# Query projections of two batches as three float32r products, with a transfer plan at another rate and a new order list

## The chip, the core and the metric

The kernel runs on one NeuronCore of a Trainium2 chip, as one program with one launch. Five engines work side by side: TensorE (PE in the profile, with its weight loads shown apart as PEld), VectorE (DVE), ScalarE (ACT), GpSimd (POOL) and SyncE (SP), which here only issues transfers. The metric is the device time of one execution in microseconds (us). Three runs of the kernel before gave a median of 582.48 us (582.31 to 582.5); the execution that was profiled took 582.31 us.

## The reference

Three layers follow each other. All inputs and outputs are float32.

```python
# 1. attention with random features: 4 batches, 8 heads, 576 positions, head size 64, 128 features
def phi(x):                                   # x = q or k, scaled by 64 ** -0.25
    h = x @ omega.T - (x * x).sum(-1, keepdims=True) / 2
    return np.exp(h - h.max(-1, keepdims=True)) / np.sqrt(128)
kv, z = phi(k).T @ v, phi(k).sum(0)           # for each batch and head
x = (phi(q) @ kv) / (phi(q) @ z + 1e-6)       # heads side by side: 2304 tokens x 512
# 2. dense layer, 512 -> 2048 -> 512
h = x @ w_in
x = (h * np.clip(h + 3, 0, 6) / 6) @ w_out
# 3. eight experts, 512 -> 1024 -> 512: each token with x @ w_skip > 0 goes to its best one
out[t] = x[t] + gate[t] * (np.maximum(x[t] @ w1[e], 0) @ w2[e])
```

The change touches the product of q with omega inside phi(q).

## The kernel before

**Attention.** Heads are taken in pairs: a pair (b, p) is batch b and two heads, one in partitions 0 to 63 and one in 64 to 127, so there are four pairs in a batch. For each pair the keys are projected in blocks of 128 positions (`nat`, L448), reduced to their maximum on DVE (L454), passed through the exponential on ACT (L469) and multiplied with v (`k_kv`, L485). The queries are projected with the features in the partitions (`q_proj`, L515): two halves of 288 columns each, and in each half two float32 matmuls, one for each head, of which one uses the array's upper 64 rows and the other its lower 64. One float32 matmul of the program stands as two MATMUL records in the trace. ACT copies the result to SBUF (L543), POOL takes the maximum over partitions (L551), DVE subtracts it (L556), ACT takes the exponential (L560), and TensorE multiplies with kv (`x_num`, L570). DVE divides (L581 to L583), TensorE transposes (L592), ACT and DVE split the result into a high and a low float32r part, `xh` (L607) and `xl` (L612).

**Dense layer.** Tokens go in five chunks of 512, 512, 256, 512 and 512. For each chunk and each of 16 slices of the hidden layer `mm1` (L712) makes three products of high and low parts, twelve float32r matmuls, and `mm2` (L743) three more for each 128 tokens. Batch 0 must be through before the first `mm1`; batches 1, 2 and 3 are worked in between the matmuls of chunks 0 to 2. In the same time ACT and DVE turn the 64-bit words in which the weights arrive into float32 and split them (L643 to L690).

**Experts.** A large block for one expert (L990 to L1072), a small one (L1157 to L1192) and a loop for what is left, which runs zero times on these inputs.

**Array modes.** TensorE runs in three ways here: over the whole array (`mm1`, `mm2`, transposes, and the fill matmuls on `idle`, L299), in two halves of 64 rows (L448, L515), and in parts of its columns (L485, L570, L1169, L1192). A change between these is called a mode change below.

**What sets the order.** All work is registered as some 2,000 numbered operations, each with an engine, a cost, a due time, what it reads and writes, and the tiles it takes from small pools. The stored list ORDER says in which order they are written into the engines' queues, and each engine works its queue in that order. `Schedule.gaps` walks the list with the planned costs; in the kernel itself its result only decides how many fill matmuls are put into the planned idle time of TensorE before projections of batch 0. The constants DMA and RATE are its latency in us and its bytes per us for transfers. The tile pool "raw" has three buffers of 576 columns, which hold k and q of the pair in work and what is loaded ahead. SP works its queue in order, so that a load which waits for a buffer holds up those behind it.

Of the kernel before, what the change touches and what calls it, by code (L numbers as in the profile page):

```python
# [51 lines left out]
MERGE = 2  # L52
VX = 2
# [200 lines left out]
def performer_moe_kernel(  # L254
# [1026 lines left out]
    def act(n):  # L1281
        return 0.09 + n * 0.84e-3
# [16 lines left out]
    def attention(b, start, period):  # L1299
        for p in range(4):  # L1300
# [12 lines left out]
            def kind(tag):  # L1313
                return "ps"
# [335 lines left out]
```

## Time and profile before

| what | value |
|---|---|
| median of 3 runs | 582.48 us |
| profiled execution, its own time | 582.31 us |
| its span, first to last instruction | 580.5 us |
| TensorE matmul busy | 565.8 us, 97% |
| VectorE busy | 423.6 us, 73% |
| ScalarE busy | 293.4 us, 51% |
| GpSimd busy | 109.4 us, 19% |
| mean granted TensorE clock | 0.993 of full speed |
| instructions in the span | 11189 |

The span is 1.8 us shorter than the execution's own time, since that includes what lies around the first and the last instruction. Matmul busy time is modelled up to the end of each matmul's pipeline, so a record of 0.39 us may follow the one before it by 0.23 us; what a matmul costs is read from the distance between starts.

### The profile page before, as it was taken

The page shows a single profiled execution, that of the slowest core. Times are in us where ns is not written, and L with a number is a line of the kernel's source. Part 1 is how long each engine was busy: PE and PEld are TensorE (multiplying, and loading weights), DVE is VectorE, ACT ScalarE, POOL GpSimd, SP SyncE. Part 2 cuts the span into 40 slices and gives each one's busy share as a digit, 9 for nine tenths or more (in the row PEclk, how much of TensorE's full clock was granted, in tenths as well). Part 3 has the DMA queues.
Part 4 walks back from the last instruction along what each step waited for, and adds up shares of the span by engine and source line. Part 5 has one row for each costly group of instructions (what it writes and reads, how often), then busy time and mean ns, then how long its engine had stood idle before and what let it go on. Part 6 is the DMA issues. An engine that isn't in the chain of part 4 may idle for free. (4 is left out here: it accounts for less than half of the span.)

```text
span 580.5 us, 11189 instructions
## 1 busy us (share of the span) xinstructions
PE 565.8 (97%) x4117; PEld 469.5 (81%) x4117; DVE 423.6 (73%) x1116; ACT 293.4 (51%) x665; POOL 109.4 (19%) x83
## 2 busy tenths in 40 slices
PE   9899999999999999999999999999999999999993
PEld 7778788888888787878988888888888888898872
DVE  5999999988752442356678886798898974599961
ACT  5999999896563533357743431321432224553310
POOL 4543023000020202023222000020020133200363
PEclk9999999999999999999999999999999999999997
DMA  8635665666565143214644243121123535274721
GB/s 318 223 106 165 204 218 180 209 194 222 159 238 153 37 137 119 60 48 129 180 144 146 74 124 101 48 92 56 35 32 112 148 92 164 84 235 126 237 65 66
DMA packets 37256, 79.52 MB, mean 137 GB/s; under 512 B 5612, under 2 KB 6252, under 8 KB 37200
## 3 DMA queue, kind: packets, MB, share of 16 engines
q1 hardware_dynamic: 35024, 74.80, 41.1%
q0 software_dynamic: 1744, 3.56, 2.1%
q8 instruction: 33, 0.54, 0.4%
q10 hardware_dynamic: 432, 0.43, 0.3%
q14 instruction: 23, 0.19, 0.1%
HBM read 63.71 MB, written 15.18 MB: 136 GB/s over the span
## 5 line engine op out<-in xcount | busy, mean ns | idle before, releaser
L743 PE MATMUL acc<-wo,gh 128*128 128x512 f32 x576 | 180.9, 395 | 0.0
L743 PEld LDWEIGHTS acc<-wo,gh 128*128 128x128 f32 x576 | 105.4, 188 | 22.3 <-issue 1.2
L763 DVE CUSTOM_DVE_ANT_0 idle<-x,wg 128x512 uint8<-128x512 f32 x162 | 112.6, 695 | 5.3 <-ACT x L749 1.5
L743 PE MATMUL acc<-wo,gl 128*128 128x512 f32 x288 | 112.3, 390 | 0.0
L551 POOL PARTITION_ALL_REDUCE mx<-pr x26 | 52.9, 2074 | 237.6 <-ACT pr L543 237.6
L727 ACT CAST gh<-g 128x512 fp32r<-128x512 f32 (+1 forms) x80 | 46.6, 584 | 97.7 <-PE acc L743 84.2
L733 DVE TENSOR_TENSOR gl<-g,gh 128x512 fp32r<-128x512 f32 (+1 forms) x80 | 51.2, 640 | 58.0 <-ACT gh L727 22.0
L718 ACT ACTIVATE g<-mm,half_t 128x512 f32<-128x512 f32 (+1 forms) x80 | 52.0, 650 | 67.5 <-DVE gl L733 36.1
L712 PE MATMUL mm<-xh,wih 128*128 128x512 f32 (+1 forms) x320 | 80.8, 374 | 0.5 <-DVE xn L583 0.5
L712 PE MATMUL mm<-xl,wih 128*128 128x512 f32 (+1 forms) x320 | 78.8, 368 | 0.0
L723 DVE SCALAR_TENSOR_TENSOR g<-g,mm 128x512 f32<-128x512 f32 (+1 forms) x80 | 49.7, 630 | 26.1 <-ACT g L718 25.8
L712 PEld LDWEIGHTS mm<-xh,wih 128*128 128x128 f32 x320 | 56.0, 188 | 12.1 <-DVE xn L583 0.7
L712 PEld LDWEIGHTS mm<-xl,wih 128*128 128x128 f32 x320 | 56.8, 188 | 10.2
L743 PEld LDWEIGHTS acc<-wo,gl 128*128 128x128 f32 x288 | 54.0, 188 | 11.6
L712 PE MATMUL mm<-xh,wil 128*128 128x512 f32 (+1 forms) x256 | 61.7, 363 | 0.0
L712 PEld LDWEIGHTS mm<-xh,wil 128*128 128x128 f32 x256 | 44.8, 189 | 7.9 <-DMA wil<-wils 0.4
L841 POOL DMA_INDIRECT tab<-rec,r_sloti x18 | 19.5, 1086 | 154.9 <-DVE rec L837 151.0
L469 ACT ACTIVATE kp<-att,kmx 128x128 f32<-128x128 f32 x130 | 38.4, 395 | 7.8 <-DVE kmx L454 6.7
L454 DVE TENSOR_REDUCE kmx<-att 128x3 f32<-128x384 f32 (+1 forms) x64 | 28.9, 484 | 12.8 <-PE att L448 12.6
L556 DVE TENSOR_TENSOR pr<-pr,mx 128x576 f32<-128x576 f32 x26 | 26.1, 1005 | 1.4 <-POOL mx L551 1.3
L668 DVE CUSTOM_DVE_ANT_0 ca<-w,ca 128x1024 uint16<-128x1024 uint16 x32 | 23.6, 741 | 3.0 <-ACT w L654 2.1
L448 PEld LDWEIGHTS att<-wb,raw 64*128 64x128 f32 x260 | 20.3, 195 | 5.6 <-ACT pr L543 1.5
(222 smaller groups left out, 777.3 us busy)
## 6 DMA issues: line engine op xcount, KB each, us to landing
wil<-wils SPq DMA_DIRECT2D x64, 256.0 KB, 2.7
w<-w_in SPq DMA_DIRECT2D x16, 512.0 KB, 4.0
w<-w_out SPq DMA_DIRECT2D x16, 512.0 KB, 3.8
out<-x SPq DMA_DIRECT2D x18, 256.0 KB, 3.6
x1d<-x SPq DMA_DIRECT2D x18, 256.0 KB, 3.8
vx<-vn SPq DMA_DIRECT2D x13, 322.5 KB, 4.5
wils<-cl SPq DMA_DIRECT2D x16, 256.0 KB, 4.2
wraw<-w SPq DMA_DIRECT2D x16, 256.0 KB, 2.9
```

The lines of the kernel that those rows point to most:

```text
L454: V.reduce_max(out=mx[:, 0:n], in_=st[key, b, p, g, h][:, 0:n * M].rearrange("p (g m) -> p g m", m=M), axis=AX.X, negate=True)
L469: A.activation(kp[:, i], ps[:, i * M:(i + 1) * M], AF.Exp, bias=mx[:, i:i + 1], scale=1.0)
L551: G.partition_all_reduce(mx, st["e", b, p, r], channels=128, reduce_op=bass_isa.ReduceOp.max)
L556: V.tensor_sub(pr, pr, st.pop(("qm", b, p, r)))
L668: V.tensor_tensor(c, c, lo, op=ALU.add)
L712: T.matmul(po, w[:, k, :], moving(x, k, c), start=(n == 0), stop=(n == 3 * KC - 1))
L718: A.activation(t, mmp[c, f][:, 0:CHS[c]], AF.Relu, bias=half_t, scale=2.0 ** -UP / 6.0)
L723: V.scalar_tensor_tensor(out=t, in0=t, scalar=1.0, in1=mmp.pop((c, f))[:, 0:CHS[c]], op0=ALU.min, op1=ALU.mult)
L727: A.copy(gh, gt[c, f])
L733: V.tensor_sub(gl, t, gh.bitcast(F32))
L743: T.matmul(accs[c, t], g[:, ts], w[:, r, f % 2, :], start=(f == 0 and j == 0), stop=(f == FT - 1 and j == 2))
L763: V.tensor_tensor_reduce(out=idle.bitcast(mybir.dt.uint8), in0=x1[i], in1=wg[:, e, :], scale=1.0, scalar=0.0, op0=ALU.mult, op1=ALU.add, a ...
```

## The change

Queries of batches 2 and 3 (`SPLIT = 2`) are projected in another form. ACT rounds omega (`wbh`) and q (`qh`) to float32r, DVE takes the rests (`wbl`, `ql`), and each half projection becomes three float32r products, wbh·qh + wbl·qh + wbh·ql, over 320 and 256 columns instead of 288 and 288. `qh` and `ql` take buffers of the pool "raw", and the load of the next pair's keys is placed behind the making of `ql`. Two constants of the plan change, some small tiles share their memory, and ORDER is another list, with new numbers because there are 18 more operations.

```diff
+SPLIT = 2
 ORDER = """
-256 257 294 295 16 1 332 333 370 258 260 296 259 31 266 268 272 263 273 261 279 274 297 280 262 281 301 298 275 264
...
+256 257 409 294 295 332 333 16 370 258 260 31 296 259 268 1 266 272 269 334 261 273 267 263 262 310 279 311 317 274
...
-    DMA, RATE, TURN, STEP, HOLD = 2.0, 0.2e6, 0.2, 0.03, 0.6
+    DMA, RATE, TURN, STEP, HOLD = 2.4, 0.4e6, 0.2, 0.03, 0.6
...
+    wbh = sm.tile([128, M], F32R, tag="wbh", name="wbh")
+    wbl = od.tile([128, M], F32R, tag="wbl", name="wbl")
...
     def q_cols(b, p, i):
+        if b >= SPLIT:
+            return (slice(0, 320), slice(320, S))[i]
         return slice(i * 384, 384 + i * 192) if (b, p) in QPE else slice(i * HS, (i + 1) * HS)
+
+    def wb_hi():
+        A.copy(wbh, wb)
+
+    def wb_lo():
+        V.tensor_sub(wbl, wb, wbh.bitcast(F32))
+
+    def q_hi(b, p):
+        st["qh", b, p] = at.tile([128, S], F32R, tag="raw", bufs=RAW, name="qh")
+        A.copy(st["qh", b, p], st["qr", b, p])
+
+    def q_lo(b, p):
+        st["ql", b, p] = at.tile([128, S], F32R, tag="raw", bufs=RAW, name="ql")
+        V.tensor_sub(st["ql", b, p], st["qr", b, p], st["qh", b, p].bitcast(F32))
...
-        if (b, p) not in QPE:
+        if b >= SPLIT:
+            qh, ql = st["qh", b, p], st["ql", b, p]
+            for j, (w, x) in enumerate(((wbh, qh), (wbl, qh), (wbh, ql))):
+                for r in range(2):
+                    T.matmul(ps[r][:, 0:n], w[half(r), :], x[half(r), c], start=(j == 0), stop=(j == 2))
+        elif (b, p) not in QPE:
             for r in range(2):
                 T.matmul(ps[r][:, 0:n], wb[half(r), :], qr[half(r), c], start=True, stop=True)
...
-            add("ACT" if b + p == 0 else "SP", SPC, -9, load_k, (), seq="sraw", w=["kr"], tl=[("raw", "k")], nbytes=S * 512)
+            add("ACT" if b + p == 0 else "SP", SPC, -9, load_k, (), seq="sraw", w=["kr"], tl=[("raw", "k")], nbytes=S * 512,
+                aft=[("ql", (b * 4 + p - 1) // 4, (p - 1) % 4)] if b * 4 + p > 4 * SPLIT else [])
...
+            fine = b >= SPLIT
+            if fine:
+                add("ACT", act(S), u, q_hi, (), r=["qr"], w=["qh"], tl=[("raw", 0), ("raw", "h")])
+                add("DVE", dve(S), u, q_lo, (), mode="x", r=["qh", "wbl"], w=["ql"], tl=[("raw", 0), ("raw", "h"), ("raw", "l")])
...
-                add("PE", 0.62, u + i, q_proj, (i,), mode="r", r=["wb", "qr"] + ["qm", "shapes"] * mine, w=[("qps", i)],
+                add("PE", 3 * (n + 32) / 2400 + 0.03 if fine else 0.62, u + i, q_proj, (i,), mode="r", r=["wb", "ql" if fine else "qr"] + ["qm", "shapes"] * mine, w=[("qps", i)],
...
+    sc.add("ACT", 0.22, 90.0, lambda: wb_hi(), r=["wb"], w=["wbh"])
+    sc.add("DVE", 0.2, 90.0, lambda: wb_lo(), mode="x", r=["wbh"], w=["wbl"])
```

Three places show how the order moves. In the changed kernel the same code stands some 3 to 33 lines further down: L472 is the old L469, L488 the old L485, L539 the old L515, L567 the old L543, L594 the old L570, L616 the old L592, L736 the old L712, L767 the old L743, and L536 is the new product.

The first is the start of ACT's queue: `pr` and `lent_h` hold projected queries, `kp` and `lent_r` exponentials of keys, `w` and `ca` weights being turned. Before:

```order
L543 ACT_TABLE_LOAD
L543 COPY pr<-mm 128x288 x3
L469 ACTIVATE kp<-att,kmx 128x128 x3
L543 COPY pr<-mm 128x288
L469 ACTIVATE kp<-att,kmx 128x128 x5
L469 ACTIVATE lent_r<-att,kmx 128x128 x3
L543 COPY lent_h<-mm 128x288
```

And in the changed kernel:

```order
L513 ACT_TABLE_LOAD
L513 CAST wbh<-wb 128x128
L472 ACTIVATE kp<-att,kmx 128x128 x7
L567 COPY pr<-mm 128x288
L567 COPY lent_h<-mm 128x288
L567 COPY pr<-mm 128x288
L567 COPY lent_h<-mm 128x288
L567 COPY pr<-mm 128x288
L567 COPY lent_h<-mm 128x288
L567 COPY pr<-mm 128x288
```

ACT begins with the rounding of omega and seven exponentials of the first pair's keys, where it began with three copies of projected queries; the copies of the first two pairs now alternate.

The second is TensorE's queue just ahead of the first `mm1`, the last products of batch 0 and the first of batch 1. Before:

```order
L570 MATMUL att<-lent_h 64x65 x20
L570 MATMUL att<-kv,pr 64x65 x20
L592 MATMUL mm<-ident,xn 128x128 x5
L515 MATMUL att<-raw,wb 128x288 x2
L448 MATMUL att<-wb,raw 128x128 x6
L515 MATMUL att<-raw,wb 128x288 x2
L448 MATMUL att<-wb,raw 128x128 x6
L712 MATMUL mm<-xh,wih 128x512 x4
```

And in the changed kernel:

```order
L616 MATMUL mm<-ident,xn 128x128 x8
L488 MATMUL att<-vx,kp 64x65 x12
L594 MATMUL att<-kv,pr 64x65 x20
L488 MATMUL att<-vx,kp 64x65 x8
L616 MATMUL mm<-ident,xn 128x128 x4
L539 MATMUL att<-raw,wb 128x288 x2
L451 MATMUL att<-wb,raw 128x128 x6
L539 MATMUL att<-raw,wb 128x288 x2
L736 MATMUL mm<-xh,wih 128x512 x4
```

Twenty more of the narrow products with v (`att<-vx,kp`) now stand ahead of the first `mm1`: 220 narrow products in all against 200, with the same 90 products of L448 and L515 on either side.

The third is TensorE's queue around one pair of batch 2 or 3; `raw`, `qh` and `ql` are queries, `wb`, `wbh` and `wbl` omega. Before:

```order
L570 MATMUL att<-kv,pr 64x65 x20
L743 MATMUL acc<-wo,gh 128x512 x2
L743 MATMUL acc<-wo,gl 128x512
L743 MATMUL acc<-wo,gh 128x512 x2
L743 MATMUL acc<-wo,gl 128x512
L592 MATMUL att<-ident,xn 128x128 x3
L515 MATMUL att<-raw,wb 128x288 x4
L448 MATMUL att<-wb,raw 128x128 x10
L485 MATMUL att<-vx,kp 64x65 x20
L712 MATMUL mm<-xh,wih 128x256 x4
```

And in the changed kernel:

```order
L594 MATMUL att<-kv,pr 64x65 x20
L536 MATMUL att<-qh,wbh 128x320 x2
L536 MATMUL att<-qh,wbl 128x320 x2
L536 MATMUL att<-ql,wbh 128x320 x2
L767 MATMUL acc<-wo,gh 128x512 x2
L767 MATMUL acc<-wo,gl 128x512
L536 MATMUL att<-qh,wbh 128x256 x2
L536 MATMUL att<-qh,wbl 128x256 x2
L536 MATMUL att<-ql,wbh 128x256 x2
L767 MATMUL acc<-wo,gh 128x512 x2
L767 MATMUL acc<-wo,gl 128x512
L616 MATMUL att<-ident,xn 128x128 x3
```

Four matmuls of 288 columns become twelve of 320 or 256, and here the two halves no longer stand together: three wide matmuls of `mm2` lie between them.

Over the whole queue of TensorE there are 83 mode changes before and 94 after; ahead of the first `mm1` there are 21 and 25. The numbers of wide, narrow, transposing and key-projecting matmuls are the same in both kernels, and fill matmuls go from 21 to 16.

## Rows read from the trace of the kernel before

**Rows 1.** The page, busy time of the engines: us, share of the span, instructions.

```profile
PE 565.8 (97%) x4117; PEld 469.5 (81%) x4117; DVE 423.6 (73%) x1116; ACT 293.4 (51%) x665; POOL 109.4 (19%) x83
```

**Rows 2.** Busy time by stage, with granted TensorE clock (1.00 is 2.4 GHz) and transfers.

```profile
core 0: us, PE busy (x) PEld busy (x) DVE busy (x) ACT busy (x) POOL busy (x), PEclk, DMA share, GB/s
0.00:48.00 48.00, 43.59 (x643) 36.40 (x644) 40.01 (x94) 40.99 (x117) 20.57 (x15) 1.00 0.63 217
48.00:130.00 82.00, 81.98 (x591) 66.47 (x592) 75.16 (x152) 77.90 (x156) 13.08 (x6) 1.00 0.61 193
210.00:330.00 120.00, 119.55 (x1129) 101.58 (x1125) 70.36 (x171) 56.77 (x154) 24.14 (x12) 1.00 0.36 108
571.00:580.50 9.50, 0.00 (x0) 0.00 (x0) 0.51 (x1) 0.00 (x0) 1.37 (x2) 0.59 0.15 59
```

**Rows 3.** Waits of TensorE, the up-projection's: us in total, times, longest.

```profile
PE mm L712 <- DVE xn L583: 0.5, 1, 0.5
```

**Rows 4.** TensorE from 222 us: start, us to modelled end, instructions.

```profile
223.40 1.08 PE L712 MATMUL mm<-xh,wil 128*128 128x512 f32 x4
224.41 0.76 PE L515 MATMUL att<-raw,wb 64*128 64x288 f32 x4
225.09 1.39 PE L485 MATMUL att<-vx,kp 128*64 128x65 f32 x40
226.41 1.20 PE L712 MATMUL mm<-xh,wih 128*128 128x512 f32 x4
```

**Rows 5.** TensorE from 289 us.

```profile
291.41 1.24 PE L515 MATMUL att<-raw,wb 64*128 64x288 f32 x8
292.58 0.73 PE L743 MATMUL acc<-wo,gh 128*128 128x512 f32 x2
...
295.25 0.64 PE L712 MATMUL mm<-xh,wil 128*128 128x256 f32 x4
295.73 0.64 PE L712 MATMUL mm<-xh,wih 128*128 128x256 f32 x4
```

**Rows 6.** TensorE from 512 us.

```profile
512.17 0.75 PE L1034 MATMUL mm<-xl,gw 128*128 128x320 f32 x4
512.75 0.75 PE L1034 MATMUL mm<-xh,gw 128*128 128x320 f32 x4
```

**Rows 7.** TensorE from 568 us.

```profile
568.51 0.62 PE L1066 MATMUL acc<-gw,xh 128*128 128x512 f32 x2
568.97 0.39 PE L1066 MATMUL acc<-gw,xl 128*128 128x512 f32 x1
```

**Rows 8.** Weight loads of the up-projection from the page, with the mean ns of one.

```profile
L712 PEld LDWEIGHTS mm<-xh,wih 128*128 128x128 f32 x320 | 56.0, 188 | 12.1 <-DVE xn L583 0.7
```

**Rows 9.** ACT in the first 50 us; idle time before, with its releaser, in brackets.

```profile
7.20 1.00 ACT L543 COPY pr<-mm 128x288 f32<-128x288 f32 x3 [3.58 <-PE mm L515]
...
9.12 1.46 ACT L469 ACTIVATE kp<-att,kmx 128x128 f32<-128x128 f32 x5
10.37 0.97 ACT L469 ACTIVATE lent_r<-att,kmx 128x128 f32<-128x128 f32 x3
...
11.40 0.81 ACT L643 ACTIVATE ca<-w 128x512 f32<-128x512 f32 x1
11.98 0.82 ACT L543 COPY lent_h<-mm 128x288 f32<-128x288 f32 x2
...
38.19 0.62 ACT L469 ACTIVATE lent_r<-att,kmx 128x128 f32<-128x128 f32 x2 [0.89 <-DVE kmx L454]
...
45.15 0.77 ACT L607 CAST xh<-mm 128x384 fp32r<-128x384 f32 x2
```

**Rows 10.** DVE's first maximum of keys.

```profile
5.74 0.76 DVE L454 TENSOR_REDUCE kmx<-att 128x2 f32<-128x256 f32 x2 [1.31 <-PE att L448]
```

**Rows 11.** TensorE at the first up-projection.

```profile
47.88 1.19 PE L712 MATMUL mm<-xh,wih 128*128 128x512 f32 x4
```

**Rows 12.** Loads of keys from the page: KB each, median us from issue to landing.

```profile
raw<-kt SPq DMA_DIRECT2D x12, 288.0 KB, 4.4
```

More of the change, by code (lines that the diff above doesn't have):

```diff
@@ L315, in performer_moe_kernel @@
     V.memset(ones, 1.0)
-    first = const.tile([128, 1], F32, name="first")
-    G.partition_all_reduce(first, idle[:, 0:1], channels=128, reduce_op=bass_isa.ReduceOp.max)
+    upper = const.tile([128, 1], F32, name="upper")
+    G.partition_all_reduce(upper, idle[:, 0:1], channels=128, reduce_op=bass_isa.ReduceOp.max)
     half_t = const.tile([128, 1], F32, name="half_t")
@@ L328, in performer_moe_kernel @@
     pidx = const.tile([128, 1], F32, name="pidx")
-    upper = const.tile([128, 1], F32, name="upper")
     thr = const.tile([128, NT // 128], F32, name="thr")
@@ L361, in performer_moe_kernel @@
     od = ctx.enter_context(tc.tile_pool(name="od", bufs=1))
-    od.tile([128, 56], F32, tag="pad", name="pad")
+    wbh = sm.tile([128, M], F32R, tag="wbh", name="wbh")
+    wbl = od.tile([128, M], F32R, tag="wbl", name="wbl")
+    od.tile([128, 16], F32, tag="pad", name="pad")
     at = ctx.enter_context(tc.tile_pool(name="at", bufs=1))
@@ L811, in route_copy @@
         V.tensor_copy(tot, ps[:, 64:64 + TPC[c] * NE].rearrange("p (n e) -> p n e", e=NE))
-        pos = sm.tile([128, TPC[c], NE], F32, tag="r_pos", name="r_pos")
+        pos = sm.tile([128, TPC[c], NE], F32, tag="r_d", name="r_pos")
         V.tensor_copy(pos, ps[:, 0:TPC[c] * NE].rearrange("p (n e) -> p n e", e=NE))
@@ L818, in route_slot @@
         tot, pos, oh, act = rt["tot"], rt["pos"], rt["oh"], rt["act"]
-        sm_ = sm.tile([128, TPC[c]], F32, tag="r_sm", name="r_sm")
+        sm_ = sm.tile([128, TPC[c]], F32, tag="r_mx", name="r_sm")
         V.reduce_sum(out=sm_, in_=rt["ex"], axis=AX.X)
@@ L868, in list_in @@
         j3 = bc(jdx.unsqueeze(2), LS)
-        exc = sm.tile([128, NE], F32, tag="l_exc", name="l_exc")
+        lw = lb["w"] = sm.tile([128, M], F32, tag="wbh", name="lw")
+        exc = lw[:, 3 * NL:3 * NL + NE]
         V.tensor_sub(exc, inc, nb)
@@ L879, in list_e @@
         ge, lt = lb["ge"], lb["lt"]
-        hit = sm.tile([128, NL], F32, tag="l_hit", name="l_hit")
+        lw = lb["w"]
+        hit = lw[:, 0:NL]
         V.reduce_sum(out=hit, in_=ge, axis=AX.X)
         V.tensor_mul(lt, ge, bc(eidx.unsqueeze(1), LS))
-        ei = sm.tile([128, NL], I32, tag="lb_e", name="lb_e")
-        eb = sm.tile([128, NL], F32, tag="l_eb", name="l_eb")
+        ei = lw[:, NL:2 * NL].bitcast(I32)
+        eb = lw[:, 2 * NL:3 * NL]
         V.reduce_sum(out=eb, in_=lt, axis=AX.X)
@@ L898, in list_r @@
         V.tensor_scalar(hit, hit, -float(TABN), float(TABN), op0=ALU.mult, op1=ALU.add)
-        ri = sm.tile([128, NL], I32, tag="lb_r", name="lb_r")
+        ri = lb["w"][:, 3 * NL + NE:4 * NL + NE].bitcast(I32)
         V.tensor_add(ri, eb, hit)
@@ L1203, in performer_moe_kernel @@
     ntot = sm.tile([128, 1], I32, tag="ntot", name="ntot")
-    ea = sm.tile([128, 1], I32, tag="ea", name="ea")
-    ra = sm.tile([128, 1], I32, tag="ra", name="ra")
-    es = sm.tile([128, 1], I32, tag="es", name="es")
-    rs = sm.tile([128, 1], I32, tag="rs", name="rs")
+    ear = sm.tile([128, 2], I32, tag="ea", name="ear")
+    ea, ra = ear[:, 0:1], ear[:, 1:2]
+    esr = sm.tile([128, 2], I32, tag="es", name="esr")
+    es, rs = esr[:, 0:1], esr[:, 1:2]
     lb = {}
@@ L1253, in list_b @@
         V.tensor_sub(rest, cnt, used)
-        nb = begun(rest, "b_nb")
-        lb["nb"], lb["inc"] = nb, prefix(nb, "b_inc")
+        nb = begun(rest, "a_oh")
+        lb["nb"], lb["inc"] = nb, prefix(nb, "a_t8")
     def expert_of(t):
@@ L1301, in attention, with add @@
             t = start + p * period + AT[f"o{b}{p}"]
-            def add(eng, cost, dt, f, a, r=(), w=(), tl=(), nbytes=0, seq=None, mode="f", over=()):
+            def add(eng, cost, dt, f, a, r=(), w=(), tl=(), nbytes=0, seq=None, mode="f", over=(), aft=()):
                 last = chain.get(seq)
@@ L1308, in add @@
                     chain[seq] = (seq, b, p)
-                sc.add(eng, cost, t + dt, lambda p=p: f(b, p, *a), mode=mode, o=[last] if last else [], r=[k if k in ("wb", "shapes") else (k, b, p) if isinstance(k, str) else (*k, b, p) for k in r],
+                sc.add(eng, cost, t + dt, lambda p=p: f(b, p, *a), mode=mode, o=[*([last] if last else []), *aft], r=[k if k in ("wb", "wbl", "shapes") else (k, b, p) if isinstance(k, str) else (*k, b, p) for k in r],
                        w=[(k, b, p) if isinstance(k, str) else (*k, b, p) for k in w] + list(over),
@@ L1352, in attention @@
                 n = c.stop - c.start
-                add("PE", 0.62, u + i, q_proj, (i,), mode="r", r=["wb", "qr"] + ["qm", "shapes"] * mine, w=[("qps", i)],
-                    tl=[("raw", 0)] + [(kind("x"), "q", r, i) for r in range(2)] + [("pr", r) for r in range(2)] +
+                add("PE", 3 * (n + 32) / 2400 + 0.03 if fine else 0.62, u + i, q_proj, (i,), mode="r", r=["wb", "ql" if fine else "qr"] + ["qm", "shapes"] * mine, w=[("qps", i)],
+                    tl=([("raw", "h"), ("raw", "l")] if fine else [("raw", 0)]) + [(kind("x"), "q", r, i) for r in range(2)] + [("pr", r) for r in range(2)] +
                     ([("qmx", g, h) for g, h in parts] if mine else []))
```

161 rows, old and new, of the table ORDER are left out of this document.

## The prediction

> **What bounds the kernel now.** I read the busy shares first. TensorE is busy for 97% of the span, ScalarE for 51% and VectorE for 73% [rows 1], so the question is where the missing 3% lie, and whether TensorE's time is work or waiting. The chain that ended last is of no help, since it holds only the last two instructions. The table by stage does [rows 2]. The reader is to see that all of TensorE's missing time lies at the two ends: 43.59 of the first 48 us are busy, 81.98 of the next 82, and then nothing is missing but 0.45 us between 210 and 330. After 571 us TensorE has no instruction, and 9.5 us of scatter and closing follow. The granted clock stands at 1.00, the 2.4 GHz level, in every stretch with matmuls. In the first stage ScalarE is busy 40.99 us of 48 and works without a break of more than 0.9 us from 7.20 us on [rows 2, 9]; there TensorE is fed by ScalarE and VectorE. From the first up-projection at 47.88 us [rows 11] on, TensorE is the bound, and its list of waits has only one entry for the up-projections, 0.5 us [rows 3].
>
> So the time is: start of the first up-projection, plus all of TensorE's work that stands behind it, plus waits, plus the tail. A change helps if it makes that work less, moves some of it ahead of 47.88 us, or lets the first up-projection start sooner. Work on other engines is hidden unless it makes TensorE wait.
>
> **The change part by part.**
>
> *The products themselves.* A pair's projection before is eight records in two halves of the array. From their start to the next group lie 291.41 to 292.58, 1.17 us [rows 5]; for four records it is 224.41 to 225.09, 0.68 us [rows 4]. The difference, 0.49 us, is two steps of two records side by side, 0.245 us each, and 0.68 - 0.49 = 0.19 us is what a visit costs beyond its work. A pair thus costs 4 x 0.245 = 0.98 us. The new product has no row. Its columns run in float32r; wide float32r matmuls start 0.145 us apart at 320 columns (512.17 to 512.75, four of them, rows 6) [rows 6] and 0.12 us apart at 256 (295.25 to 295.73, four) [rows 5]. If two heads still run side by side, a pair costs 3 x (0.145 + 0.12) = 0.795 us. Gain 0.185 us for a pair, 8 pairs: **-1.5 us**. Bounds: the fastest float32r row is 0.23 us for 512 columns (568.51 to 568.97, two) [rows 7], 0.45 ns a column, hence 0.776 us for the pair's 3 x 576 columns and -1.6 us. The other end is that the two heads take turns: 1.59 us a pair, +4.9 us. I take -1.5 because the float32 records of the same two halves do run side by side: one after the other, eight of them at 0.245 us would take 1.96 us, not 1.17.
>
> A weight load has a mean of 188 ns [rows 8]. For each head and half projection there are now three, where there were two, one for each record. Wide matmuls with a load each still start 0.12 us apart at 256 columns [rows 5], so loads of 188 ns lie beside the matmul ahead of them. The page "TensorE: Matmul & The Clock Gate" of the Trainium skill, in its Part 3 on packing small matmuls, says that a weight load overlaps with a matmul in flight only when it goes to other rows of the array. In this kernel's wide stream each load goes to the same rows, and it hides almost wholly, so the trace does not bear the rule out for float32r; the case in which it holds is priced among the rivals from the 188 ns.
>
> *Mode changes.* A visit in another mode costs 0.19 us beyond its work (above); the part at the way in shows as well where four wide matmuls after a visit take longer than 4 x 0.23. I counted 83 mode changes before and 94 after, 21 and 25 of them ahead of the first up-projection. Behind it there are 62 and 69, seven more, where the halves of a projection no longer stand together: 7 x 0.19 = **+1.3 us**. Those four ahead of it lie in time that is waited away anyway, if the start is set by ScalarE.
>
> *Work moved across the first up-projection.* Twenty narrow products now stand ahead of it. As 40 records they took 225.09 to 226.41, 1.32 us [rows 4], less 0.19 for the visit: 1.1 us that TensorE no longer does later, **-1.1 us**, if the up-projection doesn't start later for it.
>
> *The start.* ScalarE's last cast of batch 0 that the first up-projection needs begins at 45.15 and ends at 45.92 us [rows 9]. In the new order ScalarE has more ahead of that cast: six exponentials of keys of batch 1 at 0.25 us (five in 9.12 to 10.37) [rows 9], one scaling of weights at 0.58 (11.40 to 11.98) [rows 9] and a small copy of some 0.1, together 2.2 us. Against that it can begin sooner. It sat idle for 3.58 us until 7.20, waiting for the first projection of queries; now it begins with exponentials, whose first maximum is ready when VectorE's first two reductions, from 5.74 us on, have run, the first of them after some 0.4 us [rows 9, 10]. That is 6.1 us, 1.1 sooner. And idle stretches like the 0.89 us at 38.19 [rows 9] are there to be filled by the added exponentials. 2.2 - 1.1 - 0.9 = +0.2, so I take the start as unchanged, **0**. The ends are -1.1 (the sooner beginning carries through, the rest is filler) and +2.2 (nothing is won). The rounding of omega lies in ScalarE's idle time before 6.1 us.
>
> *Added work on ScalarE and VectorE.* `qh` and `ql` are eight copies and eight subtractions of 576 columns, about as long as the exponential of the same width. Between 210 and 330 us ScalarE is busy 56.77 and VectorE 70.36 of 120 us [rows 2], so this lies beside other work; **0**. Without that cover it would be some 1.2 us for a pair.
>
> *Loads and the pool of three.* `qh` and `ql` take two of the three buffers. A load of keys can go only when `ql` of the pair before is made, and a load of queries only when that pair is projected; SP stands behind either, and with it loads of low weights for the up-projection. A load of keys lands 4.4 us after its issue in the median [rows 12]. Where pairs follow each other most closely, the matmuls that the new order puts between one projection and the next make 9.7 us by the durations above, so load (4.4) and split (about 1.2) fit with some 4 us to spare; one block of keys, 2 us behind a projection, has hardly any. I take **0**, bounds 0 and +2.
>
> *The planner's constants.* They alter nothing but the number of fill matmuls (21 to 16), since the list sets the order. What they did to the list is in the terms above.
>
> Sum on the profiled execution: 582.31 - 1.5 + 1.3 - 1.1 = **581.0 us**. It lies 0.17 us under the median of the runs, which I leave, being within their spread of 0.19.
>
> **Rivals.**
>
> *The start comes sooner.* Two loads of weights no longer stand ahead of the third pair's keys and queries, and ScalarE begins 1.1 us sooner. For it: ScalarE is nearly gapless there, so an earlier beginning carries through. Against it: 2.2 us more work in the same stretch. Time: 581.0 - 1.1 = 579.9.
>
> *The start comes later; slower than before.* ScalarE does all of the 2.2 us ahead of its last cast, and the 1.1 us are lost again where it waits for the alternating copies of the second pair, whose queries come later than the first's. Place: ScalarE's queue from 6 to 46 us; price 2.2 us, 581.0 + 2.2 = 583.2. It decides from the point where the first up-projection starts later than 49.2 us, 1.3 us behind 47.88, since then all gains are used up.
>
> *Waits for q.* The two or three tightest pairs wait for loads behind the pool of three, 0.5 to 1 us each: 582.3 to 583. For it: loads with 4.4 us in the median, against a plan that reckons with faster ones. Against it: TensorE's list of waits has no transfer before.
>
> *The halves don't pack, and so the change does not do what it says.* If the two heads take turns, the product is 0.61 us dearer for a pair: 581.0 + 1.5 + 4.9 = 587.4. If they pack but each weight load of 188 ns stands before its matmul, six of them make 0.795 + 1.13 = 1.92 us a pair, and 581.0 + 1.5 + 7.6 = 590.1. This second time is what the rule in Part 3 of that page of the Trainium skill would give here. Against both: float32 records pack in the same halves, and wide loads are hidden.
>
> **How the numbers follow.** The forecast has 0.40 (own range 580.2 to 582.0), the sooner start 0.20, the later start 0.20, waits for q 0.12, turns of the heads 0.05, and standing weight loads 0.03. A difference under 0.2%, 1.2 us here, can't be told from none: under 581.3 is faster, over 583.6 slower. Faster gets the sooner start and somewhat over half of the forecast, 0.46; slower the last two, a part of the later start and a little of the waits, 0.20; 0.34 are left. The range takes in the sooner start with the 0.5 us wait gone as well, 579.4, and some less, 579.0, and the later start with waits added, up to 584.5; the cases without packing, 0.08, are left out.
>
> **What the profile after would show.** Right: the new product's records in pairs, and a visit of six of them some 0.4 us (256 columns) or 0.45 (320) plus 0.2 long; the first up-projection between 47 and 49 us; ScalarE's first exponential near 6.1 us; no transfer and no `ql` among TensorE's waits beyond 0.5 us; 9 to 10 us from the last matmul to the end. Wrong: records of one visit that follow each other instead of pairing; a first up-projection after 49.2 or before 46.5; waits of 1 us or more between 150 and 320 us; a granted clock under 1.00 before 48 us.

## The result and the profile after

The changed kernel takes 590.62 us (median of 4 runs, 589.38 to 591.91) beside 582.39 us of the kernel before on the same chip: ratio 1.0142, 95% interval 1.0119 to 1.0165. It is 1.4% slower. The forecast was 581.0, with a range of 579.0 to 584.5: wrong in sign, and far outside the range. The profiled execution was the longest of the four, 591.91 us.

The page's first line after, in the columns of [rows 1]. TensorE has 4.5 us more busy time and stays the bound; the other engines hardly changed:

```profile
PE 570.3 (97%) x4139; PEld 466.7 (79%) x4139; DVE 426.2 (72%) x1125; ACT 296.8 (50%) x674; POOL 108.7 (18%) x83
```

The table by stage after; the first two stages are among those of [rows 2], and the last is one in which TensorE had no idle time before:

```profile
0.00:48.00 48.00, 41.47 (x666) 34.57 (x668) 38.70 (x91) 42.44 (x122) 20.62 (x15) 1.00 0.70 235
210.00:330.00 120.00, 120.00 (x1179) 101.54 (x1177) 91.25 (x251) 62.05 (x164) 28.59 (x16) 1.00 0.37 111
330.00:450.00 120.00, 117.44 (x514) 94.34 (x513) 76.55 (x237) 31.21 (x63) 6.34 (x6) 1.00 0.25 64
```

No hole holds 8 us, and the granted clock is 1.00 in every stretch with matmuls, as before. The profiled execution is 9.6 us longer than the one before. Its first up-projection starts 1.0 us later. From there to the end of TensorE's last record TensorE waits 3.5 us, where it waited 0.5, and is busy for 527.9 us, where it was busy for 522.4. The largest part, 5.5 us, thus goes without idle time and without a lower clock: it is in the instructions themselves. TensorE's timeline after shows where. A group of three wide matmuls of `mm2`, two with `gh` and one with `gl` (start, us to modelled end, instructions):

```profile
424.25 0.63 PE L767 MATMUL acc<-wo,gh 128*128 128x512 f32 x2
424.72 0.40 PE L767 MATMUL acc<-wo,gl 128*128 128x512 f32 x1
424.95 0.63 PE L767 MATMUL acc<-wo,gh 128*128 128x512 f32 x2
...
425.65 0.63 PE L767 MATMUL acc<-wo,gh 128*128 128x512 f32 x2
```

The same in the kernel before:

```profile
424.15 0.62 PE L743 MATMUL acc<-wo,gh 128*128 128x512 f32 x2
...
424.83 0.62 PE L743 MATMUL acc<-wo,gh 128*128 128x512 f32 x2
...
425.51 0.62 PE L743 MATMUL acc<-wo,gh 128*128 128x512 f32 x2
```

From group to group lie 0.70 us after, 233 ns for a matmul, and 0.68 us before, 227 ns. Below, the distance from the start of one matmul to the start of the next is called its step. The grouped view (busy us, mean ns of one record) shows the change for all wide matmuls of the up- and down-projections; the first row had 395 ns before:

```profile
L767 PE MATMUL acc<-wo,gh 128*128 128x512 f32 x576 | 184.5, 401 | 0.0
L767 PE MATMUL acc<-wo,gl 128*128 128x512 f32 x288 | 113.9, 395 | 0.0
L736 PE MATMUL mm<-xh,wih 128*128 128x512 f32 x256 | 70.3, 396 | 1.0 <-ACT x L773 0.9
L736 PE MATMUL mm<-xl,wih 128*128 128x512 f32 x256 | 69.2, 392 | 0.0
L736 PE MATMUL mm<-xh,wil 128*128 128x512 f32 x192 | 52.4, 394 | 1.5 <-DMA wil<-wils 1.5
L736 PE MATMUL mm<-xh,cl 128*128 128x512 f32 x64 | 17.5, 394 | 0.0
```

Two waits in these rows are new (1.5 and 0.9 us; before there was one of 0.5 [rows 3]); the one of 1.5 us is in no other profile here. What the forecast spoke of came as follows: the first up-projection starts 1.0 us later than in [rows 11], and shortly ahead of it TensorE waits for ScalarE's copy of kv (idle time before, with its releaser, in brackets),

```profile
46.52 0.44 PE L616 MATMUL mm<-ident,xn 128*128 128x128 f32 x2 [0.54 <-ACT kv L502]
...
48.91 1.20 PE L736 MATMUL mm<-xh,wih 128*128 128x512 f32 x4
```

and a projection of 320 columns takes 0.64 us (237.94 to 238.58), one of 256 takes 0.55 (240.17 to 240.72), where four float32 records of 288 columns took 0.68 [rows 4]:

```profile
237.94 0.42 PE L536 MATMUL att<-qh,wbh 64*128 64x320 f32 x2
238.19 0.31 PE L536 MATMUL att<-qh,wbl 64*128 64x320 f32 x2
238.34 0.31 PE L536 MATMUL att<-ql,wbh 64*128 64x320 f32 x2
238.58 0.73 PE L767 MATMUL acc<-wo,gh 128*128 128x512 f32 x2
...
240.17 0.39 PE L536 MATMUL att<-qh,wbh 64*128 64x256 f32 x2
...
240.72 0.73 PE L767 MATMUL acc<-wo,gh 128*128 128x512 f32 x2
```

### The profile page after: what moved, and what is told of

It reads as the page before. It is cut to its first block, busy times and chain, and to the rows that moved or that the text cites. A ratio compares the mean times of both kernels' runs of the same rounds, so it can differ in the third digit from the quotient of the medians.

```text
span 590.1 us, 11263 instructions
## 1 busy us (share of the span) xinstructions
PE 570.3 (97%) x4139; PEld 466.7 (79%) x4139; DVE 426.2 (72%) x1125; ACT 296.8 (50%) x674; POOL 108.7 (18%) x83
## 5 line engine op out<-in xcount | busy, mean ns | idle before, releaser
L767 PE MATMUL acc<-wo,gh 128*128 128x512 f32 x576 | 184.5, 401 | 0.0
L767 PEld LDWEIGHTS acc<-wo,gh 128*128 128x128 f32 x576 | 104.9, 188 | 24.9 <-issue 1.0
L767 PE MATMUL acc<-wo,gl 128*128 128x512 f32 x288 | 113.9, 395 | 0.0
L757 DVE TENSOR_TENSOR gl<-g,gh 128x512 fp32r<-128x512 f32 (+1 forms) x80 | 53.5, 669 | 59.8 <-ACT gh L751 33.4
L742 ACT ACTIVATE g<-mm,half_t 128x512 f32<-128x512 f32 (+1 forms) x80 | 51.9, 652 | 62.1 <-PE mm L736 21.2
L736 PE MATMUL mm<-xh,wih 128*128 128x512 f32 (+1 forms) x320 | 81.2, 376 | 1.0 <-ACT x L773 0.9
L736 PE MATMUL mm<-xl,wih 128*128 128x512 f32 (+1 forms) x320 | 79.4, 370 | 0.0
L736 PEld LDWEIGHTS mm<-xh,wih 128*128 128x128 f32 x320 | 56.1, 188 | 13.8 <-ACT x L773 1.4
L736 PEld LDWEIGHTS mm<-xl,wih 128*128 128x128 f32 x320 | 56.8, 188 | 10.5
L767 PEld LDWEIGHTS acc<-wo,gl 128*128 128x128 f32 x288 | 54.1, 188 | 13.0
L736 PE MATMUL mm<-xh,wil 128*128 128x512 f32 (+1 forms) x256 | 62.6, 366 | 1.5 <-DMA wil<-wils 1.5
L736 PEld LDWEIGHTS mm<-xh,wil 128*128 128x128 f32 x256 | 44.6, 188 | 10.1 <-DMA wil<-wils 1.9
L472 ACT ACTIVATE kp<-att,kmx 128x128 f32<-128x128 f32 x130 | 39.3, 433 | 10.9 <-DVE kmx L457 10.8
L580 DVE TENSOR_TENSOR pr<-pr,mx 128x576 f32<-128x576 f32 x26 | 22.4, 878 | 3.6 <-POOL mx L575 3.5
L1069 ACT ACTIVATE gr<-mm 128x320 f32<-128x320 f32 (+1 forms) x16 | 6.6, 410 | 36.4 <-PE mm L1060 30.3
```

The source lines that it names most:

```text
L472: A.activation(kp[:, i], ps[:, i * M:(i + 1) * M], AF.Exp, bias=mx[:, i:i + 1], scale=1.0)
L580: V.tensor_sub(pr, pr, st.pop(("qm", b, p, r)))
L736: T.matmul(po, w[:, k, :], moving(x, k, c), start=(n == 0), stop=(n == 3 * KC - 1))
L742: A.activation(t, mmp[c, f][:, 0:CHS[c]], AF.Relu, bias=half_t, scale=2.0 ** -UP / 6.0)
L757: V.tensor_sub(gl, t, gh.bitcast(F32))
L767: T.matmul(accs[c, t], g[:, ts], w[:, r, f % 2, :], start=(f == 0 and j == 0), stop=(f == FT - 1 and j == 2))
```

## The experiments

Why would the same wide matmuls start farther apart? The change has an edit that looks like housekeeping, and the diff above leaves it out: the tile `first` goes and `upper` takes its place. By the allocation a tile of one float has a slot of 32 bytes, so every tile allocated behind it in `const`, `wts` and `xp` moves down by 32 bytes: the weights `wih` and `wo`, and `xh` and `xl`. The pad in `od` makes up for it, so that the later pools stay: the parts `gh` and `gl` of g, and the reloaded low weights `wil`. All of these lay at multiples of 128 bytes before; after, the first group has remainder 96 by 128 and the second still 0. (Also, `gh` and `wil` changed places, which keeps the remainder.) Of a matmul's two operands one, 128 x 128 here, is loaded by a record of its own (PEld) and is called stationary; the other, of up to 512 columns, is called moving. In `mm1` the moving operand is `xh` or `xl` and the stationary `wih` or `wil`; in `mm2` the moving operand is `wo`, the stationary `gh` or `gl`.

### The place alone: four runs

Undo it in the changed kernel, and nothing else:

```
     G.partition_all_reduce(upper, idle[:, 0:1], ...)
+    const.tile([128, 8], F32, name="spacer")
...
-    od.tile([128, 16], F32, tag="pad", name="pad")
+    od.tile([128, 8], F32, tag="pad", name="pad")
```

> The changed kernel with one unused 32-byte tile put back behind `upper`, and the pad in `od` 32 bytes smaller. No instruction differs; the weights, xh, xl and omega begin at multiples of 64 bytes again, where the changed kernel has them at 64k+32. Theory (place): wide float32r matmuls start 227 ns apart again instead of 231 to 234; some 1,750 of them, 7 to 8.5 us back: 582 to 583.5. Rival (order and waits, the new products, or the swap of `pr` with `kp` and `gh` with `wil`): no change, 590 to 591.

Measured: 583.68 us, ratio to before 1.0022 (95% interval 1.0011 to 1.0032): 7 us of the 8.2 are back. The wide rows have the means of the kernel before again (three of them):

```profile
L768 PE MATMUL acc<-wo,gh 128*128 128x512 f32 x576 | 181.6, 396 | 0.0
L768 PE MATMUL acc<-wo,gl 128*128 128x512 f32 x288 | 112.4, 390 | 0.0
L737 PE MATMUL mm<-xh,wil 128*128 128x512 f32 x192 | 51.3, 389 | 0.0
```

Do it in the kernel before, with nothing else of the change:

```
-    first = const.tile([128, 1], F32, name="first")
-    G.partition_all_reduce(first, idle[:, 0:1], ...)
+    upper = const.tile([128, 1], F32, name="upper")
+    G.partition_all_reduce(upper, idle[:, 0:1], ...)
...
-    upper = const.tile([128, 1], F32, name="upper")
...
-    od.tile([128, 56], F32, tag="pad", name="pad")
+    od.tile([128, 64], F32, tag="pad", name="pad")
```

> The kernel before with nothing of the change but the tile: `first` goes, the reduction at the start writes `upper` in its place, and the pad in `od` is 32 bytes larger, so that only the tiles behind it, weights, xh, xl, omega, move by 32 bytes. Theory (place): 7 to 8.5 us slower, 589.5 to 591; mm2 steps of 232 to 235 ns, no new waits of TensorE. Rival: 582.4, steps of 227.

Measured: 589.31 us, ratio 1.0114 (1.0100 to 1.0129). So one slot of 32 bytes costs 1.1% in a kernel without any other edit. (This time and the one before lie 0.2 us outside the ranges expected.) Its timeline says more than its time:

```profile
426.77 1.08 PE L711 MATMUL mm<-xl,wih 128*128 128x512 f32 x4
427.68 1.09 PE L711 MATMUL mm<-xh,wil 128*128 128x512 f32 x4
428.61 0.63 PE L742 MATMUL acc<-wo,gh 128*128 128x512 f32 x2
...
429.31 0.63 PE L742 MATMUL acc<-wo,gh 128*128 128x512 f32 x2
...
430.01 0.63 PE L742 MATMUL acc<-wo,gh 128*128 128x512 f32 x2
```

`xl` with `wih`, both moved, keeps 0.91 us for four; `xh` with `wil`, of which one moved, takes 0.93; `mm2`, of whose operands one moved, takes 0.70 for three.

Next, each side alone. Only `xh` and `xl` 32 bytes up (with the small tiles behind them):

```
     xp = ctx.enter_context(tc.tile_pool(name="xp", bufs=1))
+    xp.tile([128, 8], F32, name="spacer")
...
-    od.tile([128, 56], F32, tag="pad", name="pad")
+    od.tile([128, 48], F32, tag="pad", name="pad")
```

> The kernel before with only xh and xl (and the small tiles behind them) 32 bytes later, so at 64k+32; the weights stay. Theory (place of the moving operand): mm1, whose moving operand is xh or xl, steps 231 to 235 instead of 227, 768 matmuls of 512 columns x 4 to 7 = 3 to 5.4 us; mm2, whose moving operand is wo, stays at 227: 585.5 to 588. Second form of the theory (the weights are what matters): 582.4 and no step changed.

Measured: 587.25 us, ratio 1.0088 (1.0075 to 1.0101). Within one stretch `mm1` is slow and `mm2` recovers:

```profile
425.11 1.09 PE L713 MATMUL mm<-xl,wih 128*128 128x512 f32 x4
426.05 1.09 PE L713 MATMUL mm<-xh,wil 128*128 128x512 f32 x4
426.98 0.63 PE L744 MATMUL acc<-wo,gh 128*128 128x512 f32 x2
...
427.67 0.63 PE L744 MATMUL acc<-wo,gh 128*128 128x512 f32 x2
...
428.36 0.62 PE L744 MATMUL acc<-wo,gh 128*128 128x512 f32 x2
...
429.04 0.62 PE L744 MATMUL acc<-wo,gh 128*128 128x512 f32 x2
...
429.72 0.62 PE L744 MATMUL acc<-wo,gh 128*128 128x512 f32 x2
```

Four of `mm1` take 0.94 and 0.93 us; the groups of `mm2` take 0.69, 0.69, and then 0.68 each. The step follows the matmul's own operands, after a few matmuls of transition.

Only the weights 32 bytes up (`xh` and `xl` by 64, so that they stay at a multiple of 64); the first spacer stands behind `wb`, ahead of the weights:

```
+    const.tile([128, 8], F32, name="spacer")
+    xp.tile([128, 8], F32, name="spacer2")
...
-    od.tile([128, 56], F32, tag="pad", name="pad")
+    od.tile([128, 40], F32, tag="pad", name="pad")
```

> The kernel before with only the weights 32 bytes later, at 64k+32 (wih is mm1's stationary, wo mm2's moving operand); xh and xl move by 64 and stay on multiples of 64. Theory (place of the moving operand): mm2 steps 232 to 235, 864 x 6.8 = 5.9 us, mm1 stays at 227: 588 to 588.5. If the stationary's place matters too, mm1 widens as well and the sum of the whole shift comes here alone, 589.5 to 591.

Measured: 590.25 us, ratio 1.0132 (1.0117 to 1.0146), above what the moving operand alone would give. `mm1` widened too, though only its stationary has an odd place (before: 395 and 390):

```profile
L714 PE MATMUL mm<-xh,wih 128*128 128x512 f32 x256 | 71.3, 400 | 0.0
L714 PE MATMUL mm<-xl,wih 128*128 128x512 f32 x256 | 69.9, 394 | 0.0
L714 PE MATMUL mm<-xh,wil 128*128 128x512 f32 x192 | 52.3, 395 | 0.0
```

So my first form of the theory, the place of the moving operand, fell. Moving one side costs `mm1` time whichever side it is, and moving both alike costs it next to nothing (0.91 us for four): what counts is how the two stand to each other.

### Which unit, and is it the difference?

All of weights, `xh` and `xl` 64 bytes up, in the kernel before, by a spacer behind `wb`:

```
+    const.tile([128, 16], F32, name="spacer")
...
-    od.tile([128, 56], F32, tag="pad", name="pad")
+    od.tile([128, 40], F32, tag="pad", name="pad")
```

> The kernel before with the weights, xh and xl all 64 bytes later; the tiles of the later pools (the high and low parts of g, the reloaded low weights) stay. Theory A (operands that begin at multiples of 64 are fast): 582.4, no step changed. Theory B (a matmul is fast when its moving operand and its stationary stand at the same remainder by 128, slow when they don't; in the run with the weights alone moved by 32, the products of xh, then at 64 mod 128, with reloaded low weights at 0 were slow, 233 ns, which A doesn't give): xh and xl with wih stay at 227; xh with the reloaded low weights and mm2 (wo against the parts of g) go to 231 to 235; the sum like that of the run with all moved by -32, 588 to 590.

Measured: 584.39 us, ratio 1.0036 (1.0023 to 1.0049): between the two theories, and neither had its number.

```profile
423.66 1.07 PE L713 MATMUL mm<-xl,wih 128*128 128x512 f32 x4
424.57 1.08 PE L713 MATMUL mm<-xh,wil 128*128 128x512 f32 x4
425.48 0.62 PE L744 MATMUL acc<-wo,gh 128*128 128x512 f32 x2
...
428.23 0.62 PE L744 MATMUL acc<-wo,gh 128*128 128x512 f32 x2
```

From 425.48 to 428.23 us lie four groups of `mm2`, twelve matmuls: 2.75 us, 0.687 a group, 229 ns a matmul: in `mm2` a difference of 64 bytes costs a third of what 32 costs. In `mm1` it isn't so clear. `xh` and `wil` stand 64 apart here, with a mean record of 392 ns:

```profile
L713 PE MATMUL mm<-xh,wil 128*128 128x512 f32 x192 | 51.8, 392 | 0.0
```

They stand 64 apart in the run with only the weights moved as well, and there it is 395, as much as that of products 32 apart. Ahead of them run products 32 apart in that run and undisturbed ones here, so the matmuls ahead seem to count too; that was not tried.

The changed kernel with one number changed, so that the later pools stand 32 bytes lower too and all operands have remainder 96:

```
-    od.tile([128, 16], F32, tag="pad", name="pad")
+    od.tile([128, 8], F32, tag="pad", name="pad")
```

> The changed kernel with its pad in `od` 32 bytes smaller and nothing else: now the later pools, with the parts of g, the reloaded low weights and the raw inputs, stand 32 bytes lower as well, so that moving and stationary operands have the same remainder again though none of them is a multiple of 64. Theory B (only the difference counts): steps back to 227, 582.5 to 584.5 as with the tile put back. Theory A (a multiple of 64 is what counts): 590 to 592, steps of 231 to 235 everywhere.

Measured: 582.68 us, ratio 1.0008 (0.9999 to 1.0016). None of these operands is at a multiple of 64 any more, and the groups of `mm2` take 0.68 us:

```profile
421.55 0.62 PE L767 MATMUL acc<-wo,gh 128*128 128x512 f32 x2
...
422.23 0.62 PE L767 MATMUL acc<-wo,gh 128*128 128x512 f32 x2
...
422.91 0.62 PE L767 MATMUL acc<-wo,gh 128*128 128x512 f32 x2
```

So the difference counts, not the place. Which unit it is taken by stays open. Remainders by 128 fit all runs, but by the allocation the undisturbed operands of the dense layer start whole multiples of 512 bytes apart, and no run sets its operands 128 or 256 apart. Nor is a difference dearer at every width: with `xh` and `xl` moved by 32 bytes, the 64 matmuls of 256 columns of `xl` with `wih` have a mean record of 279 ns, where it is 283 before.

### The order alone, and what the products are worth

The kernel before with the changed kernel's list, less the 18 entries of `wb_hi`, `wb_lo`, `q_hi` and `q_lo` (the others renumbered), and with the new planner constants; products in float32, nothing displaced:

```
-    DMA, RATE, TURN, STEP, HOLD = 2.0, 0.2e6, 0.2, 0.03, 0.6
+    DMA, RATE, TURN, STEP, HOLD = 2.4, 0.4e6, 0.2, 0.03, 0.6
```

> The new order and planner constants with the old float32 products: the kernel before, its list replaced by the changed kernel's without the 18 added casts and subtractions; nothing is displaced. Against the changed kernel with the tile put back (583.7) it lacks the new products alone. If these are worth what the prediction said (0.185 us a pair, and a visit of four float32 records 0.68 against 0.64 and 0.555 us now that the halves stand apart), it is 1.3 to 1.5 us slower than that: 585.0 to 585.2, with the first up-projection at 48.9 us as in the changed kernel. If the products are worth nothing: 583.7. If it is the products and their waits that cost what is left: 582.4 or less.

Measured: 584.04 us, ratio 1.0033 (1.0021 to 1.0044). Beside the run with the smaller pad, on the same chip, the new products are worth 584.04 - 582.68 = 1.4 us, as forecast. Beside the run with the tile put back, which the expectation named, it is only 0.4 us, or 0.1% by the ratios (1.0033 against 1.0022); the two differ by as much as sets of runs of one kernel do (below), so that the times don't settle it, and the worth of the products is read from the rows further down. The order alone is 2 us slower than before. Its first up-projection starts at 49.01 us (before: 47.88 [rows 11]), and its up-projection has the wait for ScalarE's copy of an output tile as well (us in total, times, longest):

```profile
PE mm L712 <- ACT x L749: 0.9, 1, 0.9
```

### Two entries of the list

The copy waits for a buffer whose store stands on SP's queue behind a load that itself waits. Two entries of the list move: that store (1785) ahead of the load, and a rounding step of 1.1 us on ScalarE (50) behind the last two casts of `xh`.

```
-... 1527 1785 1788 ...          +... 1517 1785 ... 1527 1788 ...
-... 401 50 469 ... 368 ...      +... 401 469 ... 368 50 ...
```

> The changed kernel with the tile put back, and two entries of the list moved: the store of output tile 11 goes ahead of one load of low weights on SP's queue (it stood behind a load that waits for its buffer, and TensorE waited 1.1 us at 442 us for a copy that needed the buffer of that tile), and one 1.1 us step of the weight rounding on ScalarE goes behind the last two casts of xh that the first up-projection needs. Theory: 583.7 - 1.1 - 1.0 = 581.6, first up-projection at 47.9 us, no wait over 0.5 us at 442. Rival (ScalarE is the bound from 48 to 130 us, so the moved step comes back there, and the wait for the copy moves to the next buffer): 582.7 to 583.7.

Measured: 581.10 us, ratio 0.9985 (0.9973 to 0.9997). The wait at 442 us is gone, but the first up-projection did not come sooner: it starts at 49.18 us, and ScalarE now waits for TensorE's narrow products ahead of its last casts (idle time before, with its releaser):

```profile
46.02 0.27 ACT L503 COPY kv<-att 128x130 f32<-128x130 f32 x1 [0.56 <-PE att L489]
46.38 0.76 ACT L632 CAST xh<-mm 128x192 fp32r<-128x192 f32 x2
47.03 1.36 ACT L679 ACTIVATE w<-w 128x512 f16<-128x512 f32 x1
...
48.73 0.39 ACT L568 COPY pr<-att 128x288 f32<-128x288 f32 x1
```

The row at 47.03 is the moved step. TensorE no longer waits 0.54 us for the copy of kv, but the up-projection itself now waits for the copy `pr` of projected queries, which stands behind the moved step:

```profile
49.18 1.21 PE L737 MATMUL mm<-xh,wih 128*128 128x512 f32 x4 [0.33 <-ACT pr L568]
```

All four profiles with both moves have this wait, of 0.32 to 0.36 us. From TensorE's products of queries with kv ahead of it (43.81 us in the changed kernel, 44.17 here) to the first up-projection it is 5.10 us without the move and 5.01 with it: the move gains 0.1 us.

To see which move gave the gain, with the smaller pad in place of the tile, first the store alone:

> The changed kernel with the pad in `od` 32 bytes smaller (all operands at the same remainder) and, of the two moved entries of the list, only the store of output tile 11 ahead of one load of low weights. Theory: the wait of 0.9 to 1.1 us for the copy at 442 us is gone, and this alone is what the two moves gave: about 1.1 us under the kernel with the smaller pad alone, ratio to before 0.998 to 0.9995, the time 580.8 to 581.6 where before takes 581.9. Rival (the moved rounding step gave the gain): ratio 1.0005 to 1.001, as with the smaller pad alone.

Measured: 582.52 us, ratio 1.0012 (1.0001 to 1.0023). Then both moves:

> The same with both moved entries, the store and the 1.1 us rounding step behind the last casts of xh. In the run with both moves the first up-projection still began at 49.2 us: ScalarE was free earlier and waited 0.6 us for TensorE's narrow products. Theory (TensorE's own queue ahead of the first up-projection sets the start, so the rounding step's place gives nothing): within 0.3 us of the kernel with the store alone, first up-projection after 48.5 us. Rival (ScalarE sets the start): 1.0 us less than that, first up-projection near 47.9 us.

Measured: 583.21 us, ratio 1.0017 (1.0005 to 1.0028), first up-projection at 49.59 us. Neither move lowered the time, so the 0.9985 was in doubt. The two versions with both moves, side by side on one chip:

> The kernel with the tile put back and both moved entries a second time, beside its twin with the smaller pad on one chip: the two differ in addresses alone, all operands at remainder 0 by 128 here and at 96 in the twin. On two chips their ratios to before were 0.9985 and 1.0017. Theory (only the difference of the remainders counts): equal within 0.1%, both 0.999 to 1.001 here, and the earlier difference came from the chips. Rival (remainder 0 is better than 96): this one 0.2 to 0.3% faster than the twin here too, ratio 0.998 to 0.9995.

> The twin, with the smaller pad in `od` in place of the tile put back. Theory: equal to the run beside it within 0.1%. Rival: 0.2 to 0.3% slower than it, ratio to before 1.001 to 1.002.

Measured: 582.94 us, ratio 1.0015 (0.9999 to 1.0031), and 583.10 us, ratio 1.0007 (0.9998 to 1.0016). They agree within their intervals, so no advantage of remainder 0 over 96 is shown. The gain of 0.15% did not come back; that it came from the chips is not borne out either, since this second set ran on the same chip as the first 0.9985. The intervals of single sets are thus narrower than what one set differs from the next by, and no version here is shown to beat the kernel before.

## Why the prediction was wrong, point by point

**The step that failed** is the one that wasn't taken: the sum has no term for the removed tile. It took TensorE's wide matmuls over at their old durations, as work that no edit touches, and gave nothing, without a reason, to the edit of the tile that does. The mechanism is in no term and no rival. Worked out from the rows: the mean records are longer by 5 ns in 576 and 288 (`mm2`, 401 against 396, 395 against 390) and by 1, 2, 5 and 4 in 256, 256, 192 and 64 (`mm1`, against 395, 390, 389 and 390 with the tile put back), 6.3 us together. The times give 7 to 8: 590.6 against 583.7 and 582.7. The products, which the forecast was about, are not the cause. But with the place mended the kernel is still not faster than before (1.0022 and 1.0008), so a second step was off, that of the order.

**The products, -1.5:** right by the rows. The halves pack as forecast. With halves apart a pair takes 0.64 + 0.55 us, where the order alone takes twice 0.69 (256.31 to 257.00 for one):

```profile
256.31 0.76 PE L515 MATMUL att<-raw,wb 64*128 64x288 f32 x4
257.00 0.73 PE L743 MATMUL acc<-wo,gh 128*128 128x512 f32 x2
```

0.19 us a pair against the forecast 0.185, so 1.5 us for eight pairs. The times are too coarse for it: 1.4 us beside one run and 0.4 beside another.

**Standing weight loads, 590.1, 0.03:** the time came within 0.5 us of this rival, and the rival is wrong all the same. It needs 1.92 us for a pair; the rows show 1.19. By the rule in Part 3 of the page "TensorE: Matmul & The Clock Gate" of the Trainium skill the six loads would stand; here they don't, as the rows of `qh` and `ql` above show. A time that fits is no evidence for its mechanism until the rows of the place are read. The turns of the heads fall with it.

**Order: mode changes +1.3, moved work -1.1, start 0:** together +0.2; the order alone measured +2. The start is 1.1 us of it (1.0 in the changed kernel), within the ends named (-1.1 to +2.2), and another 0.9 us is the wait for the copy, which no term has. That the time with the place mended, 582.7 to 583.7, lies about the 583.2 of the rival of the later start is luck: that rival has a delay of 2.2 us and no wait for an output tile. Of its reasons, ScalarE's first exponential is there at 5.58 us, sooner than the forecast 6.1, and the sooner beginning did not carry through. The forecast had counted the twenty moved products as won, if the start doesn't move, and the mode changes beside them as lying in time that is waited away anyway. In the profile after, TensorE waits for nothing from 43.06 us to the first up-projection but the 0.54 us for ScalarE's copy of kv, so both engines set it: the products fill TensorE's queue, and taking 1.1 us off ScalarE ahead of the last casts moved the wait to another copy of ScalarE's and gained 0.1 us. How the order's cost splits among mode changes and moved work was not separated.

**Loads and the pool of three, 0:** right where it was placed. TensorE's waits name no `ql`, `qh` or `raw` of batches 2 and 3. The new waits lie elsewhere, at 384 us for a load of low weights and at 449 us for the copy that needs a buffer, behind loads and stores of SP's queue that the sum did not follow. The first, of 1.5 us, is in no other profile here.

**ScalarE and VectorE, 0:** right. In 210 to 330 us they are busy 62.05 and 91.25 of 120.

**Left open.** Why the wait for the copy could be removed and the time not fall. In three of the five profiles with the store moved, TensorE waits near 110 us for ScalarE's queries, 0.4 to 0.7 us; the repetitions of the kernels with both moves don't have this wait. Waits of 0.2 to 0.3 us at the experts' products that no engine or transfer ends stand in most profiles with the store moved, but in the changed kernel and in that with the tile put back as well, so the store does not bring them. One kernel, the one with both moves, had ratios of 0.9985 and 1.0015 in two sets of runs, so differences of up to 0.3% between sets are not explained here; those of 0.9% and more, on which the cause rests, are well above, while the 0.36% of the run with a difference of 64 and the 0.33% of the order alone stand on their rows more than on their times. And the start varies more with the new list: 48.5 to 51.9 us in nine profiles (48.51 with the store alone, 51.90 in the repetition), against 47.6 to 48.4 in five with the old one.

## What to carry to other kernels

Read a diff for what it does to addresses: a tile dropped or added ahead of large operands moves them all, and no view of the profile names the cause. When TensorE is busy nearly throughout at full clock and the time still rises, compare the start-to-start distance of one unchanged form of matmul in both traces before anything else. And where matmuls of 512 columns fill the time, try a pad that puts moving and stationary operands at the same remainder by 128 bytes (here by 512 too): it gave 1.3% here. At 256 columns a difference of 32 bytes did no harm, so compare before you move.

## What the runs showed of the hardware

The step of float32r matmuls of 512 columns by the difference of the start addresses of moving and stationary operand, counted from a multiple of 512 bytes; each from the timelines above:

| difference, bytes | step, ns | where |
|---|---|---|
| 0, both at remainder 0 by 128 | 227 | before: `mm2` (0.68 for three); run with only `xh`, `xl` moved: `mm2` (0.68 for three, from the third group on) |
| 0, both at remainder 96 | 227 | run with pad 8: `mm2`; displaced kernel before: `xl` with `wih` (0.91 for four) |
| 64 | 229 | all 64 up: `mm2` (2.75 us for twelve); in `mm1` not settled, see there |
| 32, either operand being the higher | some 233 | changed kernel: `mm2` (0.70 for three); only `xh`, `xl` moved: `mm1` (0.94 and 0.93 for four) |

It is 1 to 3% of a matmul, invisible in TensorE's busy share, which is 97% before and after, and it costs over 1% here, where such matmuls fill the time. What in the chip makes it was not tried.
